# Three stages on one core: every step's place, engine and buffer given by a list instead of by ranks and a planner

## The chip, the core and the metric

The kernel runs on one core of a Trainium2 chip. A core has TensorE (PE in the profile; its weight loads are PEld), VectorE (DVE), ScalarE (ACT), GpSimd (POOL) and SyncE (SP, which only issues transfers). The engines run their own instruction lists in order and wait for each other by semaphores. The metric is the device time of one execution in microseconds (us).

## The reference

Attention whose scores count only where query and key fall into the same bucket (the signs of six projections), and behind it a feed-forward block with an exact GELU:

```python
batch, n_heads, seq, head_dim = (4, 8, 768, 64)
q_bits = (np.einsum('bhsd,dk->bhsk', q, proj) > 0).astype(np.int64)
k_bits = (np.einsum('bhsd,dk->bhsk', k, proj) > 0).astype(np.int64)
mask = q_bucket[:, :, :, None] == k_bucket[:, :, None, :]
scores = scale * np.matmul(q, k.transpose(0, 1, 3, 2))
scores = np.where(mask, scores, -1000000000.0)
scores = scores - np.max(scores, axis=-1, keepdims=True)
attn = np.exp(scores)
attn = attn / (np.sum(attn, axis=-1, keepdims=True) + 1e-09)
attn_out = np.matmul(attn, v)
# x: (B * S, H * D) = (3072, 512); w_in 512 x 2048, w_out 2048 x 512, arriving as 64-bit floats
h = x @ w_in
g = 0.5 * h * (1.0 + erf(h * inv_sqrt2))
out = g @ w_out
```

## The kernel before, in words

The work is cut into 3604 steps. A step is a few instructions of one engine (`emit`), with the steps it needs, the ring of buffers it takes a place from, and the engines on which it may run with a cost for each (`ways`). Some steps, such as a copy or a scaling, may run on VectorE, ScalarE or GpSimd, and a few moves inside SBUF may also be a transfer of SyncE.

Per batch there are 8 heads, two to a pair; per head 6 units of 128 queries. A head's steps load `raw`, round it to `Aq` (L418 or ScalarE's L415, out of `rawe` or `raw`, with the scale `fold`), take what is left over (`Bq`, `Bk`), move halves into `Bk`, `Ak` and `Bq`, project them (L765 to L767 for batch 0, L841 and L842 later), and write the signs as mask rows into `Aq` and `Ak`. A unit is a score product on TensorE (four matmuls, L889, into one of two buffers `s`), a minimum on VectorE (L892), the exponential on ScalarE (L897, into `p`), and then for batch 0 transposes on TensorE with copies into `pt` (L947, L418 or L415), for the other batches the row sum's scaling (`rows<-rows`) and reciprocal (L906), the weights' high half (`hl` or `wbits` from `p`) and low half (L912), and a transposing transfer. The third buffers of `p` and of `hl` are cut out of `wbits`, so their writes carry that name as well. A pair ends with the values' product (L1027 or L1036) and the two halves of `x`.

The weights arrive in pieces, are decoded on VectorE (L527, L532, L537) and scaled. The feed-forward runs in groups of 8 blocks of hidden features for 256 rows: the hidden product (L1239, into one of four buffers `hp`), its evacuation (L1249), GELU (L1274), the high half `g` (L418 or L415) and low half (L1296), and the output product (L1318), then a drain (L1345, L415 or L418) and the store.

The order comes from `Plan.order`, a list planner inside the program: it goes through modelled time with its own costs, hands each free engine the ready step with the lowest rank, and gives a buffer out as it comes free. Ranks are the step's key, a place in the sequence of units shifted by a number of the table `PAR` by the step's kind, class of head and engine. The steps are then emitted in the order of their modelled starts; that order is each engine's instruction list. `flips` and `hashes` are small constants that the heads of batches 1 to 3 use for their masks.

Of the kernel before, what the change touches and what calls it, by code (L numbers as in the profile page):

```python
# [19 lines left out]
P = 128  # L20
TC = 256
# [5 lines left out]
TABLE = 1.39  # L27
CLASSES = ((3, 3, 4, 4, 0, 0, 0, 0), (5, 5, 1, 1, 1, 1, 1, 1), (2, 2, 2, 2, 2, 2, 2, 2))
TURN = 0.11
# [4 lines left out]
PAR = dict(DR_ACT=576.84, DR_DVE=-551.41, SI0=-589.8, SI1=230.04, SI2=-34.64, SI_ACT=-397.26, SI_DVE=-373.75, SI_Pool=-360.2, Z=-61.67, VS0=-433.73, H0=378.62, HL=565.17, VS=-224.84, G2=593.89, HQ=458.56, VQ=-575.62, in0=-255.08, out0=-600, in1=-380.24, out1=295.33, in2=-124.92, out2=-97.71, in3=235.25, out3=-400.5, H1=176.86, H2=542.46, H3=-37.15, H4=458.07, H5=179.41, H6=-511.06, H7=-405.9, MEV=57.33, MGE=-266.31, MSP=582.63, V0=403.75, QK0=240.49, QK1=-248.37, QK2=252.72, MX0=-152.71, MX1=62.08, MX2=-495.94, EX0=75.03, EX1=-181.85, EX2=-102.35, NR0=-144.91, NR1=-247.83, NR2=-577.15, HI0=-417.18, HI1=25.44, HI2=-381.41, LO0=-449.91, LO1=202.06, LO2=376.24, PV0=514.02, PV1=-31.15, PV2=-408.84, TR0=172.3, TR1=-600, TR2=-12.3, V1=-391.11, V2=-325.43, Sin0=526.4, Sin1=-364.12, Sin2=-600, Sin3=277.83, Sout0=-418.02, Sout1=289.1, Sout2=0.64, Sout3=401.64, Lin=-412.45, Pin=231.92, Qin=421.02, Cin=-141.85, Min=-383.86, Lout=-95.97, Pout=107.03, Qout=-175.48, Cout=-318.56, Mout=-147.01, G0=145.57, G1=316.52, G3=502.99, G4=274.38, G5=-52.33, G6=280.57, G7=-451.2, DUP0=-368.48, DUP1=309.05, DUP2=-147.15, LOW0=-74.43, LOW1=400.08, LOW2=-437.3, PRJ0=505.26, PRJ1=-443.97, PRJ2=-573.45, MSK0=-333.44, MSK1=-332.99, MSK2=574.02, DI_ACT=484.2, DI_DVE=198.9, DI_Pool=586.97, WS_ACT=-377.49, WS_DVE=-492.68, WS_Pool=75.03, WH_ACT=-183.8, WH_DVE=254.94, WH_Pool=-132.94, WL_ACT=564.2, WL_DVE=-390.67, WL_Pool=47.05, VH_ACT=332.87, VH_DVE=273.75, VH_Pool=272.39, MV_SP=462.36, MV_ACT=561.02, MV_DVE=187.65, MV_Pool=8.43, LO_ACT=144.07, LO_DVE=-389.23, LO_Pool=-404.23, RND_ACT=-149.62, RND_DVE=-392.64, RND_Pool=-598.96, MSK_ACT=-95.97, MSK_DVE=256.26, MSK_Pool=357.17, HI_ACT=-170.11, HI_DVE=575.2, HI_Pool=368.91, EV_ACT=-392.64, EV_DVE=600, EV_Pool=-334.15, GH_ACT=-383.86, GH_DVE=-207.4, GH_Pool=11.14, RB=-383.49, RS_ACT=406.61, RS_DVE=127.79, RS_Pool=-283.07, XH_ACT=257.16, XH_DVE=206.23, XH_Pool=441.23, XL_DVE=471.07, XL_Pool=-504.86, DUP3=-510.21, DUP4=61.31, DUP5=122.24, EX3=518.86, EX4=293.1, EX5=-530.77, HI3=130.65, HI4=104.05, HI5=600, LO3=-280.76, LO4=-212.73, LO5=56.13, LOW3=-499.53, LOW4=-471.64, LOW5=90.57, MSK3=445.61, MSK4=-85.72, MSK5=-557.26, MX3=-600, MX4=-401.44, MX5=-600, NR3=-216.85, NR4=-574.93, NR5=-600, PRJ3=-473.92, PRJ4=-5.94, PRJ5=1.03, PV3=-599.87, PV4=288.41, PV5=-253.14, QK3=341.47, QK4=536.61, QK5=517.19, SI3=266.44, SI4=573, SI5=-495, TR3=-44.12, TR4=170.66, TR5=-130.38, V3=-546.29, V4=-68.24, V5=-362.38, Linb=-179.56, Loutb=-390.67, Pinb=-106.09, Poutb=-600, Qinb=395.7, Qoutb=248.99, Cinb=-157.9, Coutb=-372.14, Minb=-262.42, Moutb=-159.34, MVf_SP=192.7, MVf_ACT=537.16, MVf_DVE=-141.85, MVf_Pool=6.51, LOf_ACT=319.76, LOf_DVE=-589.84, LOf_Pool=-50.91, RNDf_ACT=600, RNDf_DVE=91.75, RNDf_Pool=-552.12, MSKf_ACT=-231.23, MSKf_DVE=461.34, MSKf_Pool=200.2)  # L34
HOPX = {"PE": -0.04, "DVE": -0.09, "ACT": 0.12, "Pool": 0.03, "SP": 0.88}
# [19 lines left out]
class Plan:  # L55

    HOP = {"PE": 0.2, "DVE": 0.2, "ACT": 0.14, "Pool": 0.07, "SP": 0.03, "none": 0.0}
    ANY = ("hp", "sign")
    SAME = {"PE": 0.0, "DVE": 0.14, "ACT": 0.14}
    START = {"DVE": 4.2, "Pool": 3.3, "SP": 1.2, "ACT": 4.3}
    QUEUE = 2.0  # L70
    PORT = 0.1
    SWITCH = ((0, -0.08, 0.1), (0, 0, 0.1), (0.13, 0.07, 0))
    WINDOW = 3.413
    YIELD = 160.0
    SLACK = {"PE": 0.6, "SP": 1.0}

# [20 lines left out]
    def slack(self, now, of, to_pe):  # L97
        late = now >= self.YIELD and of != "none"
        return late * max(self.SLACK["PE"] * to_pe, self.SLACK["SP"] * (of == "SP"))

    def order(self):
        users, left, ready = {}, {}, {}
        queues = {}
        for s in self.steps:
            left[s] = len(s.needs)
            for n in s.needs:
                users.setdefault(n, []).append(s)
            for e in s.ways:
                ready.setdefault(e, [])
            if s.takes:  # L110
                queues.setdefault(s.takes, []).append(s)
        at = {}
        head = {name: 0 for name in queues}
        waiting = set()
        events = []

        def enlist(s):
            if s.takes in queues and s.takes not in self.ANY and queues[s.takes][head[s.takes]] is not s:
                waiting.add(s)
                return  # L120
            for e in s.ways:
                ready[e].append(s)

        for s in self.steps:
            if not left[s]:
                enlist(s)
        free_at = {e: 0.0 for e in ready}
        free_at.update(self.START)
        dma_at, table = 0.0, "exp"
        port_at, port_of = 0.0, None  # L130
        warm, window, busy = False, 0, {}
        mode = 0
# [1277 lines left out]
```

## Time and profile before

| | us |
|---|---|
| median of 3 runs (lowest, highest) | 868.42 (868.17, 868.68) |
| the profiled execution | 868.76 |
| its span, first to last instruction | 866.8 |
| TensorE busy | 836.1 (96%) |
| VectorE busy | 669.8 (77%) |
| ScalarE busy | 589.2 (68%) |
| GpSimd busy | 214.4 (25%) |

Busy time is that in which at least one instruction of the engine ran; matmuls overlap each other, so a mean duration times a count is more than the busy time. The shares are means over stages with different work, and the section on rows below therefore shows them by stretch.

### The profile page before, as it was taken

The numbers are of one execution on the slowest core, as the hardware profiler recorded it, in microseconds if no ns is written. First come the engines' busy times: TensorE is split into PE (matmuls) and PEld (weight loads), VectorE is DVE, ScalarE is ACT, GpSimd is POOL, SyncE is SP. The second block draws the span as 40 slices with busy tenths as digits, with TensorE's granted clock in tenths as the row PEclk, the third lists the DMA queues.
The fourth block names the chain that finished last, engine by engine and source line by source line (L and its number), as shares of the span: only waits on it lengthen the run. The fifth ranks groups of instructions, "written<-read, shape, count | busy, mean of one in ns | idle before, by whom it ended". The sixth has DMA issues, their size and how long they took to land.

```text
span 866.8 us, 16831 instructions
## 1 busy us (share of the span) xinstructions
PE 836.1 (96%) x6428; PEld 608.4 (70%) x6428; DVE 669.8 (77%) x1285; ACT 589.2 (68%) x1012; POOL 214.4 (25%) x232
## 2 busy tenths in 40 slices
PE   4898998999999999999999999999999999999998
PEld 2675766776777686887777677777767877676663
DVE  6999989999999999978998998798978752212122
ACT  5888887777788878787877868667868642223321
POOL 4543231313431315222212214214225300000000
PEclk9999999999999999999999999999999999999999
DMA  7755453564597999788988798788877970000000
GB/s 253 218 194 162 126 152 98 152 149 107 119 198 153 195 177 206 162 149 151 198 173 159 173 177 172 148 170 169 172 167 128 152 152 2 25 1 25 2 25 24
DMA packets 271439, 119.91 MB, mean 138 GB/s; under 512 B 228928, under 2 KB 253504, under 8 KB 271360
## 3 DMA queue, kind: packets, MB, share of 16 engines
q1 hardware_dynamic: 271104, 118.85, 62.7%
q8 instruction: 50, 0.82, 0.4%
q14 instruction: 29, 0.24, 0.1%
q10 hardware_dynamic: 256, 0.00, 0.0%
HBM read 41.95 MB, written 6.29 MB: 56 GB/s over the span
## 4 chain that ended last, share of the span: by engine, by line
PE 64%; DVE 2%; DMA 0%; ACT 0%; issue 0%; DVEq 0%; ACTq 0%
PE hp L1318 24%; PE hp L1239 23%; PE s L889 9%; PE hp L1036 7%; PE hp L842 1%; PE hp L841 1%; DVE s L892 1%; DMA pt<-wbits 0%; DVE wbits L912 0%; DVE hl L912 0%; DVE Bq L819 0%; DVE g L418 0%; DVE vhl L689 0%; ACT L897 0%; ACT p L897 0%
## 5 line engine op out<-in xcount | busy, mean ns | idle before, releaser
L1239 PE MATMUL hp<-x,Win 128*128 128x256 f16 x2304 | 268.2, 273 | 0.5 <-DVE o L1345 0.3
L1318 PE MATMUL hp<-Wout,g 128*128 128x512 f16 x1152 | 266.8, 380 | 0.2 <-DVE g L1296 0.2
L1239 PEld LDWEIGHTS <-Win 128*128 128x128 f16 x2304 | 219.5, 98 | 41.9 <-issue 13.2
L892 DVE TENSOR_SCALAR_CACHE_REDUCE s<-s 128x768 f32<-128x768 f32 x192 | 182.1, 963 | 17.9 <-PE s L889 17.5
L1318 PEld LDWEIGHTS <-g 128*128 128x128 f16 x1152 | 106.2, 98 | 125.3 <-issue 13.4
L897 ACT ACTIVATE p<-s,rows 128x768 f32<-128x768 f32 x147 | 132.3, 901 | 48.4 <-DVE s L892 25.0
L889 PE MATMUL s<-Ak,Aq 128*128 128x384 f32 x360 | 138.2, 384 | 6.6 <-ACT p L897 6.1
L1249 ACT ACTIVATE h<-hp,ffs 128x512 f32<-128x512 f32 x96 | 65.6, 684 | 102.6 <-PE hp L1239 102.0
L889 PE MATMUL s<-Bk,Bq 128*128 128x384 f32 x360 | 121.4, 337 | 0.0
L418 DVE TENSOR_SCALAR g<-h,ffs 128x512 f16<-128x512 f32 x36 | 19.3, 537 | 96.0 <-PE hp L1318 78.1
L1296 DVE SCALAR_TENSOR_TENSOR g<-h,ffs,g 128x512 f16<-128x512 f32 x96 | 72.5, 771 | 25.9 <-ACT g L415 23.8
L889 PEld LDWEIGHTS s<-Ak,Aq 128*128 128x128 f32 x360 | 68.0, 189 | 22.1 <-ACT p L897 14.0
L1036 PE MATMUL hp<-pt,vhl 128*64 128x256 f16 x1296 | 76.1, 274 | 0.0
L1036 PEld LDWEIGHTS <-vhl 128*64 128x64 f16 x1296 | 68.6, 110 | 8.7 <-issue 8.0
L889 PEld LDWEIGHTS s<-Bk,Bq 128*128 128x128 f32 x360 | 68.3, 190 | 1.1
L912 DVE SCALAR_TENSOR_TENSOR wbits<-p,rows,wbits 128x768 f16<-128x768 f32 x60 | 62.5, 1046 | 3.8 <-POOL wbits L418 2.9
L897 ACT ACTIVATE wbits<-s,rows 128x768 f32<-128x768 f32 x45 | 40.4, 898 | 11.2 <-DVE s L892 5.6
L1274 ACT ACTIVATE h<-h 128x2048 f32<-128x2048 f32 (+1 forms) x25 | 46.1, 1843 | 0.4
L947 PE MATMUL hp<-ident,p 128*128 128x128 f32 x288 | 40.8, 275 | 2.6 <-DVE pt L418 1.9
L912 DVE SCALAR_TENSOR_TENSOR hl<-p,rows,hl 128x768 f16<-128x768 f32 x39 | 39.3, 1012 | 1.5 <-POOL hl L418 1.2
L947 PEld LDWEIGHTS hp<-ident,p 128*128 128x128 f32 x288 | 32.9, 141 | 8.1 <-DVE pt L418 2.5
L415 ACT ACTIVATE pt<-hp 128x384 f32<-128x384 f32 x75 | 33.8, 490 | 6.5 <-PE hp L947 6.2
(194 smaller groups left out, 1099.0 us busy)
## 6 DMA issues: line engine op xcount, KB each, us to landing
raw<-qk SPq DMA_DIRECT2D x28, 384.0 KB, 4.0
vraw<-v SPq DMA_DIRECT2D x28, 384.0 KB, 4.1
wbits<-w_in SPq DMA_DIRECT2D x16, 512.0 KB, 4.7
wbits<-w_out SPq DMA_DIRECT2D x16, 512.0 KB, 4.5
out<-o SPq DMA_DIRECT2D x11, 512.0 KB, 3.0
Bq<-Aq SPq DMA_DIRECT2D x22, 192.0 KB, 2.9
Bk<-Bq SPq DMA_DIRECT2D x18, 192.0 KB, 3.1
Bk<-Aq SPq DMA_DIRECT2D x17, 192.0 KB, 2.9
```

The costliest lines, as they stand in the source:

```text
L415: nc.scalar.activation(out=out, in_=in_, func=func, scale=scale, bias=bias)
L889: nc.tensor.matmul(to, x, y, start=k == 0, stop=k == 1)
L892: nc.vector.tensor_scalar(out=both(sp), in0=both(sp), scalar1=BIG / 2, scalar2=None, op0=ALU.min, op1=ALU.min, accum_out=nb,)
L897: nc.scalar.activation(out=buf(ex).rearrange("p (b k) -> p b k", b=2), in_=both(sp), func=AF.Exp, scale=-1.0, bias=nb, accum_out=sums[:, t ...
L912: nc.vector.scalar_tensor_tensor(out=buf(hi)[:, 1], in0=buf(ex), scalar=r, in1=buf(hi)[:, 0], op0=ALU.mult, op1=ALU.subtract,)
L947: nc.tensor.transpose(buf(step[0])[:, (k - k0) * P : (k - k0 + 1) * P], buf(ex)[:, words(k)], ident32,)
L1036: nc.tensor.matmul(pv[j * D : (j + 1) * D], buf(vh)[:, tv, kt, j * D : (j + 1) * D], buf(holds[j][0])[:, tp * KT + kt, :nt], start=kt == 0 ...
L1239: nc.tensor.matmul(buf(pair[0])[:, j * ch[1] : (j + 1) * ch[1]], win_hl[:, f0 // WB1, tw, pr, f0 % WB1 : f0 % WB1 + P], x[:, tx, pr, : ch[1]],
L1249: nc.scalar.activation(out=bufs["h"][0][:, 2 * fp : 2 * fp + 2, :nt], in_=buf(pair[0])[:, : 2 * nt].rearrange("p (j k) -> p j k", j=2), fu ...
L1274: nc.scalar.activation(out=h, in_=h, func=AF.Gelu)
L1296: nc.vector.scalar_tensor_tensor(out=gt[:, 1, s2, :nt], in0=h[:, s2, :nt], scalar=sg, in1=gt[:, 0, s2, :nt], op0=ALU.mult, op1=ALU.subtract,)
L1318: nc.tensor.matmul(buf(banks[u]), gt[:, tg, f, u * P : (u + 1) * P], wout_hl[:, ft // UT, tw, ft % UT], start=fresh and f == ti == 0, stop ...
```

## The change

`PAR`, its shifts and the whole of the planner's simulation go. In their place stands `ORDER`, a text of three characters for each of the 3604 steps: two give the step's place, one its engine and the number of its buffer. `Plan.order` reads it, sorts the steps by place and checks that each comes behind what it needs and that its buffer is free. The steps, their instructions and what they need are the same; where each stands, and on which of its engines, is another.

```diff
-PAR = dict(DR_ACT=576.84, DR_DVE=-551.41, SI0=-589.8, ...)
+ENGINES = ("PE", "DVE", "ACT", "Pool", "SP", "none")
+CODE = "ABCDEFGHIJKLMNOPQRSTUVWXYZabcdefghijklmnopqrstuvwxyz0123456789+-"
+ORDER = (
+    "CKYASIAEgAXCAagAyAA1gBMABPgBpABwIB4ICCACJICZICmICtIBigADgAIIALQAJQANQAKIAMIAOoAVBAZQAPAAWQAbQAcIAgAAlIApQAuoA2AA8QA0DA4Q"
...
     def order(self):
-        users, left, ready = {}, {}, {}
-        queues = {}
+        assert len(ORDER) == 3 * len(self.steps)
         for s in self.steps:
...
+            high, low, way = (CODE.index(c) for c in ORDER[3 * s.seq : 3 * s.seq + 3])
+            s.start = 64 * high + low
+            s.engine = ENGINES[way // 8]
+            s.cost = s.ways[s.engine][0]
+            s.slot = way % 8 if s.takes else None
+        steps = sorted(self.steps, key=lambda s: s.start)
...
-        sp = add("PE", 0.785, scores, t - PAR[f"QK{cl}"], made, takes="s")
-        mx = add("DVE", 0.876, least, t - PAR[f"MX{cl}"], [sp])
+        sp = add("PE", 0.785, scores, t, made, takes="s")
+        mx = add("DVE", 0.876, least, t, [sp])
```

The lines of the changed kernel have lower numbers; by the kernel before, its L375 is L418 (a scaling or copy of `affine`), L396 is L439, L441 is L484, L484 is L527, L685 is L728, L776 is L819, L849 is L892, L863 is L906, L869 is L912 and L1017 is L1060.

VectorE at the start of the program, before. `Aq_89` is the first head's rounded operand, `rawe` its data, `flips` the constants out of the transfer `off`, `Bq` and `Bk` what is left over, and `Win` the first weights:

```order
L370 TENSOR_SCALAR praw<-praw 128x6
L373 CAST first_hi<-praw 128x12
L375 TENSOR_TENSOR first_lo<-praw,first_hi 64x12 x2
L484 TENSOR_SCALAR flips<-off 64x1
L484 TENSOR_SCALAR flips<-flips 32x1 x3
L418 TENSOR_SCALAR Aq_89<-rawe_121,fold 128x768
L439 TENSOR_TENSOR Bk_92<-rawe_121,Aq_89 64x768
L728 SCALAR_TENSOR_TENSOR Bq_91<-rawe_121,Aq_89 64x768
L439 TENSOR_TENSOR Bk_96<-raw_80,Aq_93 64x768
L728 SCALAR_TENSOR_TENSOR Bq_95<-raw_80,Aq_93 64x768
L527 TENSOR_SCALAR Win<-wbits 128x1024
```

The same place of VectorE's list now:

```order
L327 TENSOR_SCALAR praw<-praw 128x6
L330 CAST first_hi<-praw 128x12
L375 TENSOR_SCALAR Aq_89<-rawe_121,fold 128x768
L332 TENSOR_TENSOR first_lo<-praw,first_hi 64x12 x2
L685 SCALAR_TENSOR_TENSOR Bq_91<-rawe_121,Aq_89 64x768
L396 TENSOR_TENSOR Bk_92<-rawe_121,Aq_89 64x768
L375 TENSOR_SCALAR Aq_93<-raw_80,fold 128x768
L441 TENSOR_SCALAR flips<-off 64x1
L441 TENSOR_SCALAR flips<-flips 32x1 x3
L396 TENSOR_TENSOR Bk_96<-raw_80,Aq_93 64x768
L685 SCALAR_TENSOR_TENSOR Bq_95<-raw_80,Aq_93 64x768
L375 TENSOR_SCALAR Ak_90<-sign_72 12x768
```

The rounding of the first head moved ahead of `first_lo` and `flips`, the second head's came over from ScalarE, and the mask row `Ak_90` from GpSimd stands ahead of the decoding.

VectorE in the middle of the program, before, in the stretch that leads to the left-over part `Bq0` of one head. `wbits` and `hl` are halves of the attention weights, `rows` the row sums, `s0` and `s1` the score buffers:

```order
L892 TENSOR_SCALAR s1_63,rows_99<-s1_63 128x2x384
L892 TENSOR_SCALAR s0_62,rows_99<-s0_62 128x2x384
L912 SCALAR_TENSOR_TENSOR wbits_61<-p0_68,rows_99,wbits_61 128x768
L906 RECIPROCAL rows_99<-rows_99 128x1 x2
L418 TENSOR_SCALAR hl0_70<-wbits_61,rows_99 128x768
L418 TENSOR_SCALAR Aq0_89<-raw0_80,fold_130 128x768
L912 SCALAR_TENSOR_TENSOR hl0_70<-wbits_61,rows_99,hl0_70 128x768
L819 SCALAR_TENSOR_TENSOR Bq0_91<-raw0_80,fold_130,Aq0_89 128x768
```

The same place now:

```order
L375 TENSOR_SCALAR wbits_61<-wbits_61,rows_99 128x768
L375 TENSOR_SCALAR rows_99<-rows_99 128x1
L863 RECIPROCAL rows_99<-rows_99 128x1
L375 TENSOR_SCALAR hl0_70<-p1_69,rows_99 128x768
L869 SCALAR_TENSOR_TENSOR wbits_61<-wbits_61,rows_99 128x768
L869 SCALAR_TENSOR_TENSOR hl0_70<-p1_69,rows_99,hl0_70 128x768
L863 RECIPROCAL rows_99<-rows_99 128x1
L849 TENSOR_SCALAR s1_63,rows_99<-s1_63 128x2x384
L869 SCALAR_TENSOR_TENSOR wbits_61<-p0_68,rows_99,wbits_61 128x768
L776 SCALAR_TENSOR_TENSOR Bq0_91<-raw0_80,fold_130,Aq0_89 128x768
```

High halves (`TENSOR_SCALAR` into `wbits` and `hl`) and a scaling of `rows` stand among VectorE's own work. They came from GpSimd, whose list has 84 rows instead of 224; its last rows before the final branch were these:

```order
L418 TENSOR_SCALAR Aq1_93<-sign0_72,flips_157 12x768
L418 TENSOR_SCALAR Ak1_94<-sign0_72,flips_157 12x768
L418 TENSOR_SCALAR wbits_61<-p1_69,rows_99 128x768
L418 TENSOR_SCALAR wbits_61<-wbits_61,rows_99 128x768
L418 TENSOR_SCALAR hl1_71<-p1_69,rows_99 128x768
```

and are now these, which stand much earlier in the program:

```order
L375 TENSOR_SCALAR Ak1_94<-sign0_72,flips_157 12x768
L375 TENSOR_SCALAR rows_99<-rows_99 128x1
L375 TENSOR_SCALAR g_1656<-h_1655,ffs_108 128x512
L375 TENSOR_SCALAR hl1_71<-wbits_61,rows_99 128x768
L375 TENSOR_SCALAR Bq0_91<-Aq0_89 64x768
```

Of GpSimd's work behind the attention of batch 0 little is left; its work up to there is nearly what it was.

## Rows read from the trace of the kernel before

**Rows 1.** Busy time by stretch: start:end length, busy us (instructions) by engine, clock, DMA.

```profile
6.00:164.00 158.00, 138.62 (x996) 102.34 (x997) 147.92 (x285) 129.14 (x264) 54.65 (x53) 1.00 0.53 166
164.00:700.00 536.00, 534.28 (x4268) 397.08 (x4268) 481.34 (x933) 412.04 (x689) 156.64 (x164) 1.00 0.83 165
700.00:868.00 168.00, 163.18 (x1167) 109.01 (x1165) 38.54 (x63) 46.51 (x58) 0.01 (x1) 1.00 0.10 26
```

**Rows 2.** Chain that ended last, one piece: start us, us, what.

```profile
401.84 1.41 PE s L889 x8
```

**Rows 3.** Busy time of four pieces of 50 us.

```profile
200.00:250.00 50.00, 49.41 (x394) 35.99 (x393) 46.84 (x99) 37.69 (x65) 20.11 (x20) 1.00 0.61 123
250.00:300.00 50.00, 49.37 (x386) 35.97 (x384) 48.26 (x92) 41.20 (x67) 12.99 (x14) 1.00 0.90 180
300.00:350.00 50.00, 49.85 (x394) 35.72 (x393) 47.44 (x92) 39.01 (x73) 18.11 (x16) 1.00 0.91 190
...
400.00:450.00 50.00, 49.96 (x398) 37.77 (x395) 47.91 (x94) 37.82 (x69) 10.13 (x12) 1.00 0.88 174
```

**Rows 4.** Start, in order of time: start us, us, engine line op, tiles.

```profile
0.74 0.40 SPq L707 DMA_DIRECT2D rawe<-qk  x1
...
5.67 0.17 DVE L373 CAST first_hi<-praw 128x12 fp32r<-128x12 f32 x1
...
7.88 0.15 DVE L484 TENSOR_SCALAR flips<-off 64x1 f32<-64x1 f32 x1 [1.60 <-DMA off<-offset]
...
8.57 0.62 DVE L418 TENSOR_SCALAR Aq<-rawe,fold 128x768 fp32r<-128x768 f32 x1
...
16.22 0.52 PE L889 MATMUL s<-Ak,Aq 128*128 128x384 f32 x1
```

**Rows 5.** Instructions on tile rawe until 8 us: landing of its transfer.

```profile
DMA to landing us min/median/max: 3.5/3.5/3.5
```

**Rows 6.** VectorE's groups until 164 us: shapes xcount, busy us, mean ns, idle before.

```profile
L418 DVE TENSOR_SCALAR pt<-hp 128x384 f32<-128x384 f32 x21 | 11.2, 548 | 0.7 <-PE hp L548 0.5 <-PE hp L947 0.2
```

**Rows 7.** VectorE's groups of the whole span.

```profile
L1296 DVE SCALAR_TENSOR_TENSOR g<-h,ffs,g 128x512 f16<-128x512 f32 x96 | 72.5, 771 | 25.9 <-ACT g L415 23.8
...
L912 DVE SCALAR_TENSOR_TENSOR wbits<-p,rows,wbits 128x768 f16<-128x768 f32 x60 | 62.5, 1046 | 3.8 <-POOL wbits L418 2.9 <-ACT wbits L415 0.6
...
L418 DVE TENSOR_SCALAR g<-h,ffs 128x512 f16<-128x512 f32 x36 | 19.3, 537 | 96.0 <-PE hp L1318 78.1 <-ACT h L1274 17.8
...
L418 DVE TENSOR_SCALAR wbits<-p,rows 128x768 f16<-128x768 f32 x17 | 10.4, 614 | 0.5 <-DMA pt<-wbits 0.4
...
L418 DVE TENSOR_SCALAR Ak<-sign,flips 12x768 fp32r<-12x768 f32 x6 | 5.2, 868 | 0.2
...
L418 DVE TENSOR_SCALAR rows<-rows 128x1 f32<-128x1 f32 x34 | 5.0, 148 | 8.3 <-ACT p L897 6.0 <-ACT wbits L897 1.8
...
L418 DVE TENSOR_SCALAR Bk<-Bq 64x768 fp32r<-64x768 f32 x1 | 0.6, 557 | 0.0
```

**Rows 8.** Lines L912 and L1296 behind 30 us: ns min/median/max, first and last start.

```profile
L912 DVE SCALAR_TENSOR_TENSOR wbits<-p,rows,wbits x60: 991/1014/1633, 222.7 to 704.6; 128x768 f16<-128x768 f32 x60
...
L1296 DVE SCALAR_TENSOR_TENSOR g<-h,ffs,g x96: 730/746/1396, 176.3 to 853.2; 128x512 f16<-128x512 f32 x96
```

**Rows 9.** End, in order of time.

```profile
847.54 0.49 DVE L418 TENSOR_SCALAR g<-h,ffs 128x512 f16<-128x512 f32 x1 [14.39 <-PE hp L1318]
847.94 1.41 DVE L1296 SCALAR_TENSOR_TENSOR g<-h,ffs,g 128x512 f16<-128x512 f32 x2
...
863.22 0.69 ACT L415 ACTIVATE o<-hp,ffs 128x512 f32<-128x512 f32 x1 [15.40 <-PE hp L1318]
```

**Rows 10.** TensorE from 330 to 347 us, in order of time.

```profile
334.40 1.47 PE L1318 MATMUL hp<-Wout,g 128*128 128x512 f16 x6
...
336.40 2.76 PE L1318 MATMUL hp<-Wout,g 128*128 128x512 f16 x12
...
339.70 2.12 PE L1318 MATMUL hp<-Wout,g 128*128 128x512 f16 x9
```

More of the change, by code (lines that the diff above doesn't have):

```diff
@@ new lines, in order @@
+            high, low, way = (CODE.index(c) for c in ORDER[3 * s.seq : 3 * s.seq + 3])
[4 more added lines that the diff above has]
+        steps = sorted(self.steps, key=lambda s: s.start)
+        free = {(name, k) for name, slots in self.rings.items() for k, _ in slots}
+        for s in steps:
+            assert all(n.start < s.start for n in s.needs), (s.seq, "comes before what it needs")
+            if s.takes:
+                free.remove((s.takes, s.slot))
+            for hold in s.frees:
+                hold["left"] -= 1
+                if not hold["left"]:
+                    free.add((hold["holder"].takes, hold["holder"].slot))
@@ L233, in tile_bucket_attention_moe @@
+        return steps
 @with_exitstack
@@ L430, in affine_on @@
         return {
-            e: (affine_cost(e, n, pointer) + more - less * (e == "Pool"), PAR[f"{name}_{e}"]) for e in ("ACT", "DVE", "Pool")
+            e: (affine_cost(e, n, pointer) + more - less * (e == "Pool"), 0.0) for e in ("ACT", "DVE", "Pool")
         }
     def subtract_on(name, n):
-        return {e: (subtract_cost(e, n), PAR[f"{name}_{e}"]) for e in ("DVE", "Pool")}
+        return {e: (subtract_cost(e, n), 0.0) for e in ("DVE", "Pool")}
     def subtract(engine, out, in0, in1):
@@ L515, in load @@
                     )
-                loads.append(add("SP", 1.93, load, key + d * step - PAR["L" + name], takes="wraw"))
+                loads.append(add("SP", 1.93, load, key + d * step, takes="wraw"))
             def decode(n_op, f=f, loads=loads):
@@ L692, in low @@
             )
-        raw = add("SP", 1.43, load, key - PAR["VQ"], takes="vraw")
+        raw = add("SP", 1.43, load, key, takes="vraw")
         hi = add(affine_on("VH", S, True), 0, high, key, [raw, scaled], takes="vhl", port=True)
@@ L733, in add_low @@
             if scale:
[L734 removed]
+                return add("DVE", subtract_cost("DVE", S), scaled, key, [hi], port=True)
             box = []
@@ L745, in head_early @@
         top, end = slice(0, D), slice(D, P)
-        raw = add("SP", 1.43, load, key - PAR["HQ"], takes="rawe" if b == 0 and h % 2 == 0 else "raw")
+        raw = add("SP", 1.43, load, key, takes="rawe" if b == 0 and h % 2 == 0 else "raw")
         hi = add(affine_on(f"RND{first}", S, True), 0, high, key, [raw, *clear], port=True)
@@ L821, in low @@
             )
-        raw = add("SP", 1.43, load, key - PAR["HQ"], takes="rawe" if b == 0 and h % 2 == 0 else "raw")
+        raw = add("SP", 1.43, load, key, takes="rawe" if b == 0 and h % 2 == 0 else "raw")
         hi = add(affine_on(f"RND{first}", S, True), 0, high, key, [raw, *clear], port=True)
-        lo = add("DVE", subtract_cost("DVE", S), low, key + PAR[f"LOW{cl}"], [hi], port=True)
+        lo = add("DVE", subtract_cost("DVE", S), low, key, [hi], port=True)
         free(raw, [lo])
@@ L851, in sign @@
                 )
-            box.append(add("PE", 0.08 + 0.92e-3 * (c1 - c0), project, key + PAR[f"PRJ{cl}"], [space, hashed], takes="hp"))
+            box.append(add("PE", 0.08 + 0.92e-3 * (c1 - c0), project, key, [space, hashed], takes="hp"))
             products += box
-            below = add("ACT", affine_cost("ACT", c1 - c0), lower, key + PAR[f"PRJ{cl}"], box[:1])
-            signs.append(add("DVE", subtract_cost("DVE", c1 - c0) - 0.07, sign, key + PAR[f"PRJ{cl}"], [below], port=True))
+            below = add("ACT", affine_cost("ACT", c1 - c0), lower, key, box[:1])
+            signs.append(add("DVE", subtract_cost("DVE", c1 - c0) - 0.07, sign, key, [below], port=True))
             free(box[0], signs[-1:])
```

322 lines of the change are left out of this document (136 added, 186 removed).

## The prediction

> **What bounds the kernel now.** I read the stretches first, then the start instruction by instruction, then the groups by line. The stretches [rows 1] show three stages. From 6 to 164 us (the attention of batch 0, ahead of the first hidden product) VectorE is busy 147.92 of 158 us and TensorE only 138.62: VectorE carries this stage, and 19.4 of TensorE's idle microseconds lie here. From 164 to 700 us TensorE is busy 534.28 of 536 us: it idles 1.7 us, at the full granted clock, so there is nothing to win in it by order alone. VectorE is busy 481.34 us (90%) there, ScalarE 412.04, GpSimd 156.64. After 700 us only the feed-forward products are left, TensorE has no gap before its last matmul, and behind that stand a drain of 0.69 us at 863.22 [rows 9] and its store, and both orders end with such a pair. So a new order can win in the first stage alone, and it can lose in the second, where a late VectorE, ScalarE or transfer becomes a gap on TensorE that nothing covers.
>
> **What the change does.** TensorE has the same 10,998 rows, in another order. 140 instructions leave GpSimd (rows of the order: 224 to 84), 121 rows more stand on VectorE, 50 on ScalarE; 19 transfers inside SBUF leave SyncE's queue for an engine. Counted up to the first hidden product on TensorE, VectorE has 230 instructions instead of 240 there; what GpSimd gives up it gives up almost wholly behind that point.
>
> **First stage, the start.** VectorE finishes its cast at 5.84 us, then makes two small corrections and waits for a tiny transfer before `flips`, which starts at 7.88; the first rounding of a head, `Aq`, starts at 8.57 [rows 4]. The head's data were issued at 0.74 [rows 4] and took 3.5 us to land [rows 5], so at 4.2 us they were there. In the new order `Aq` stands right behind the cast, and `flips`, whose first reader is a head of batch 1, comes after the second head's `Aq`. `Aq` can start at about 5.85: 2.7 us earlier. Behind it hang the moves, the projection, the signs and the first score matmul, at 16.22 us [rows 4]; in the new order only one head is projected ahead of it, so it should come at least as much earlier. I take 2.7 us.
>
> **First stage, VectorE's load.** Eight copies of transposed weights (`pt`, 548 ns each [rows 6]) go from VectorE to ScalarE: 8 x 0.548 = 4.4 us. ScalarE idles 158 - 129.14 = 28.9 us in the stage [rows 1] and takes them. The other edits are a few short forms each way, which I cost at nothing and leave 1.5 us of either sign for. Together 7.1 us, if VectorE bound the stage at every moment. It idles 10.1 us in it, so I take 6. Bounds: 12 us won, if half of that idle time goes too; 2 us lost, if the copies on ScalarE hold up exponentials that the next scores wait for.
>
> **Second stage, VectorE's load.** Moved onto VectorE, at the durations of [rows 7]: 43 scalings of a row sum at 148 ns, 6.4 us; 17 weights' high halves (`wbits<-p`) at 614, 10.4 us; 18 more of the same form from or into other buffers, 11.1 us; 31 operand moves, masks and roundings of 768 elements, between 557 and 868 ns, taken at 650, 20.2 us; five `g` at 537, 2.7 us; against it two output drains that leave, at 0.69 us [rows 9] 1.4 us. Sum 49 us. Two things come off. Neighbouring instructions overlap: three whose single durations are 0.49, 0.75 and 0.75 us stand from 847.54 to 849.35, 1.81 us instead of 1.99 [rows 9], some 0.09 us a joint. At 0.08 us for 119 instructions more this is 9 us. And VectorE's instructions are stretched where GpSimd works beside them: L912's commonest form has a median of 1014 and a mean of 1046 ns, with a longest of 1633; L1296 has 746, 771 and 1396 [rows 7, 8]. Mean less median, times the counts, is 60 x 0.032 + 96 x 0.025 = 4.3 us for these two; with the three other forms of L912 and `g` I take 8 us, most of which goes with GpSimd's work. So VectorE's need in the stage is about 481 + 49 - 9 - 8 = 513 us of 536, 96%; 530 at the most, 500 at the least.
>
> The Trainium skill ("SBUF — State Buffer", Who interferes with whom) says that a VectorE instruction in a two-port mode, or with two SBUF inputs, and a GpSimd instruction shut each other out for a whole instruction. The trace agrees in direction: 1.63 us against a median of 1.01 [rows 8]. By that rule some of VectorE's idle time before instructions would go as well, and its need would be nearer 500 than 513 us; by the rows it is 513. The forecast is the same by both, since TensorE sets the stage's end; only the chance of the slower rival would halve.
>
> **What 96% costs TensorE.** The kernel before has stretches like that. In the four 50 us pieces where VectorE is busiest (46.84, 48.26, 47.44 and 47.91 us) TensorE idles 0.59, 0.63, 0.15 and 0.04 us [rows 3]: 1.41 of 200 us. Over 536 us this makes 3.8 us; 1.7 are there already, so the stage becomes 2 us longer. Bounds: at the worst piece's rate 6.8, which is 5 longer; at the best's 0.4, which is 1 shorter.
>
> **Changes of kind on TensorE.** Counted in its two orders, TensorE goes 386 instead of 319 times from one kind of product to another, since scores come singly between shorter runs of feed-forward products. From 334.40 to 336.40 stand six output products and four score matmuls, from 336.40 to 339.70 twelve and four [rows 10]: six products are 1.30 us, so four score matmuls with the way there and back are 0.70. Eight in one piece take 1.41 [rows 2]. A change costs nothing that shows; I take 0, at most 0.02 us each, 1.3 us.
>
> **Transfers.** Nineteen fewer moves lie in SyncE's queue, ahead of transposes that TensorE reaches many microseconds later; VectorE and ScalarE pay for them above. At the start the third piece of weights is now issued behind loads that wait for their buffers; its reader, the second decoding, stands behind five minimum searches on VectorE in both orders. I cost both at nothing; if that cover failed, the second decoding would wait, and with it a sum of squares that no score waits for.
>
> **Sum.** Against the profiled execution, 868.76 us (span 866.8 and 1.96 around it): -6 in the first stage, +2 in the second, 0 elsewhere: 864.8. That execution stands 0.34 above the median, 868.42; so 864.4 against the median.
>
> **Rivals.**
> - *The load takes the place of the order (slower).* VectorE becomes the bound between 164 and 700 us. The busiest piece of the trace shows what it reaches, 48.26 of 50 us, 96.5% [rows 3]; 536 us at that rate hold 517 us of work. Above 517 the stage grows: at 530 (no relief from GpSimd, little overlap) to 549, 13 us, and with the 6 us of the first stage the kernel ends at +7; at 525 to 544, +2. In its middle about 872. For it: every piece of the stage, not one in three, would be this dense, and the score chain (matmul, VectorE's minimum, exponential, buffer free) has two score buffers only. Against it: 513 lies below 517, and GpSimd's stretching goes. The Trainium skill ("Perfetto Trace Analysis", Optimizing Scalar/DVE Operations) advises to take work off a saturated VectorE, to ScalarE or even GpSimd; the change goes the other way. By that advice the result is this rival's; in the trace VectorE at 96% cost TensorE 0.63 of 50 us at the most. Chance 0.25.
> - *No difference.* The first stage gains 3 and the second loses 3: within 0.2% of 868.4. For it: both terms are a few microseconds and of opposite sign. Chance 0.17.
> - *The first stage gains all it can.* 7.1 us and half of VectorE's 10.1 us of idle time there, and the second stage loses nothing: 856.5. For it: scores come singly and are spread, so that VectorE finds the next one ready; against it: something of the idle time is the chain's own. Chance 0.13.
> - That the list doesn't do what it says I give no chance: the instructions' order shows it.
>
> **How the numbers follow.** The forecast, 864.4, has 0.45 and its own range 860.5 to 866.5 (gain of 4 to 9, loss of 1 to 5, not both ends at once). A change below 0.2%, 1.7 us, can hardly be told from none here. Faster: 0.45 + 0.13 = 0.58; same 0.17; slower 0.25. The range that leaves 2 in 10 out goes down to the fullest gain's edge, 857, and up to the slower rival a little beyond its middle, 873.
>
> **What would show it.** In the changed kernel's profile: `Aq` on VectorE before 6.5 us and the first score matmul by 13.5; the first hidden product at 156 to 160 us instead of 164; after it VectorE busy 500 to 520 us in as long a stretch, GpSimd under 30, L1296's mean near 750 ns; TensorE's gaps there 2 to 6 us together, ended mostly by VectorE's or ScalarE's score steps. I would be wrong in the first stage if the first hidden product doesn't come earlier, in the second if TensorE's gaps behind it sum to over 7 us, or to under 1.

## The result and the profile after

The changed kernel takes 874.24 us (median; 873.06 to 874.81) against 868.29 (867.66 to 868.68) for the kernel before: ratio 1.0067, 95% interval 1.0050 to 1.0085, so 5.8 us slower where 4 us faster was forecast. Its profiled execution took 874.51 us, its span 872.7.

The stretches of the changed kernel (length; busy us and instructions of PE, PEld, DVE, ACT and POOL; granted clock; DMA share; GB/s), which answer to [rows 1]:

```profile
6.00:164.00 158.00, 139.52 (x986) 104.50 (x987) 140.73 (x274) 128.38 (x267) 47.79 (x49) 0.96 0.58 166
164.00:700.00 536.00, 531.87 (x4250) 393.63 (x4250) 495.10 (x1031) 451.86 (x735) 17.78 (x18) 1.00 0.76 155
700.00:868.00 168.00, 168.00 (x1192) 111.98 (x1191) 48.20 (x84) 54.14 (x71) 0.00 (x0) 1.00 0.14 34
```

TensorE's gaps in the second stretch are as forecast: 536 - 531.87 = 4.1 us. The first stretch is not as forecast. VectorE, which carried it, is busy 7 us less than before, yet TensorE is only 0.9 us further, at a clock of 0.96. The start went as forecast (VectorE and TensorE in order of time; start, length), as against 8.57 and 16.22 in [rows 4]:

```profile
5.88 0.62 DVE L375 TENSOR_SCALAR Aq<-rawe,fold 128x768 fp32r<-128x768 f32 x1
...
12.82 0.66 PE L846 MATMUL s<-Ak,Aq 128*128 128x384 f32 x1 [2.08 <-DVE Ak L375]
```

So what was won by then is lost between 13 and 164 us. The waits from 30 to 170 us (what waited, for what; us in total, times, longest) name it:

```profile
ACT sign L727 <- PE hp L724: 8.9, 3, 8.4
...
DVE Wout L484 <- DMA wbits<-w_out: 7.5, 1, 7.5
...
PE hp L722 <- DVE rb L1023: 7.1, 1, 7.1
```

The longest wait of each line belongs to one event. VectorE in order of time, and below it TensorE:

```profile
46.18 0.95 DVE L685 SCALAR_TENSOR_TENSOR Bq<-raw,Aq 64x768 fp32r<-64x768 f32 x1
54.60 0.69 DVE L484 TENSOR_SCALAR Wout<-wbits 128x1024 int32<-128x1024 int32 x1 [7.47 <-DMA wbits<-w_out]
55.21 0.16 DVE L375 TENSOR_SCALAR sums<-sums 128x4 f32<-128x4 f32 x1
55.28 0.48 DVE L1023 SCALAR_TENSOR_TENSOR rb<-hp,s_v,rb 128x256 f32<-128x256 f32 x1
```

```profile
48.27 0.49 PE L904 MATMUL hp<-ident,p 128*128 128x128 f32 x3
55.82 0.65 PE L722 MATMUL hp<-Aq,first_lo 128*44 128x512 f32 x1 [7.06 <-DVE rb L1023]
```

A decoding of weights (L484) stands on VectorE ahead of `rb`, which empties a buffer `hp` that TensorE wants next. Nobody needs the decoded weights soon; all that stands behind the decoding is late. And the clock falls (stretches of 4 us, columns as above):

```profile
48.00:52.00 4.00, 0.76 (x6) 0.49 (x4) 0.00 (x0) 0.87 (x2) 1.55 (x1) 0.89 1.07 254
52.00:56.00 4.00, 0.18 (x1) 0.18 (x2) 1.40 (x5) 0.00 (x0) 0.00 (x0) 0.50 0.14 53
56.00:60.00 4.00, 4.00 (x16) 2.04 (x17) 4.00 (x7) 1.94 (x4) 0.00 (x0) 0.50 0.14 43
60.00:64.00 4.00, 4.00 (x32) 2.77 (x29) 1.91 (x4) 2.11 (x5) 0.00 (x0) 0.83 0.89 249
```

After TensorE has stood idle, 4 us and more of its work run at 0.50, the lower of its two levels (1.2 of 2.4 GHz). A smaller stop of the same sort follows at 102.7 us (clock 0.72 from 104 to 108), behind another decoding's second part (VectorE in order of time):

```profile
100.28 1.23 DVE L489 SCALAR_TENSOR_TENSOR Win<-wbits,Win 128x1024 int32<-128x1024 int32 x1 [1.69 <-DMA wbits<-w_out]
```

This one decodes `w_in` and waits for a piece of `w_out`, which it doesn't read.

**Which transfer did the decoding wait for?** It reads two pieces of `wbits`. SyncE's queue issued them and others so (start, length):

```profile
42.33 0.37 SPq L470 DMA_DIRECT2D wbits<-w_in  x1
42.74 0.47 SPq L671 DMA_DIRECT2D Bq<-Aq  x1
43.32 0.53 SPq L578 DMA_DIRECT2D vraw<-v  x1
43.94 0.76 SPq L664 DMA_DIRECT2D rawe<-qk  x1
44.75 0.48 SPq L671 DMA_DIRECT2D Ak<-Aq  x1
45.29 0.58 SPq L470 DMA_DIRECT2D wbits<-w_out  x1
```

The landings of the first and the last (KB, us from issue to landing):

```profile
wbits<-w_in SPq DMA_DIRECT2D x1, 512.0 KB, 4.9
...
wbits<-w_out SPq DMA_DIRECT2D x1, 512.0 KB, 9.3
```

The decoding's own last piece is the one issued at 42.33, landed at 42.33 + 4.9 = 47.2. The one it waited for, landed at 54.6, is a piece of the next decoding. `wbits` has three places. By ORDER this decoding's pieces lie in places 0 and 2, the next one's in place 1, between them, and the decoding reads them through one strided view:

```
halves = wbits.rearrange("p (s f t) -> p s f t", f=512, t=2)[:, at : a + b - at + 1 : abs(a - b)]
```

With a step of 2 the view's range takes in place 1, and the instruction list has three transfers to wait for, where the decoding before it has two:

```
L484 TENSOR_SCALAR Wout<-wbits 128x1024 [waits DMAHW6_49,DMAHW4_49]
L484 TENSOR_SCALAR Wout<-wbits 128x1024 [waits DMAHW7_49,DMAHW4_49,DMAHW1_49]
```

(the third decoding, and the fourth, which is the one at 54.60). Both kernels have five decodings with places 0 and 2. In the kernel before, all five have three transfers in their lists too, but the piece between had always landed in time: this is the longest wait of a decoding for a transfer (VectorE's waits; us in total, times, longest):

```profile
DVE Wout L527 <- DMA wbits<-w_in: 0.2, 1, 0.2
```

In the changed kernel three of the five have a transfer into place 1 issued shortly before or among their parts.

### The profile page after: what moved, and what is told of

Read it like the earlier page. It is cut to its first block, busy times and chain, and to the rows that moved or that the text cites. A ratio compares the mean times of both kernels' runs of the same rounds, so it can differ in the third digit from the quotient of the medians.

```text
span 872.7 us, 16560 instructions
## 1 busy us (share of the span) xinstructions
PE 840.2 (96%) x6428; PEld 610.3 (70%) x6428; DVE 686.7 (79%) x1394; ACT 635.9 (73%) x1073; POOL 68.5 (8%) x81
## 4 chain that ended last, share of the span: by engine, by line
PE 78%; DVE 10%; ACT 5%; DMA 3%; issue 2%; POOL 0%; SPq 0%; ACTq 0%; DVEq 0%; POOLq 0%
PE hp L1196 26%; PE hp L1275 24%; PE s L846 12%; PE hp L993 7%; PE hp L984 3%; DVE s L849 3%; PE hp L904 2%; ACT p L854 2%; DMA pt<-wbits 1%; DMA wbits<-w_out 1%; DVE wbits L869 1%; DVE hl L869 1%; PE hp L798 1%; PE hp L799 1%; ACT pt L372 1%
## 5 line engine op out<-in xcount | busy, mean ns | idle before, releaser
L1275 PE MATMUL hp<-Wout,g 128*128 128x512 f16 x1152 | 276.3, 380 | 0.0
L1196 PE MATMUL hp<-x,Win 128*128 128x256 f16 x2304 | 272.7, 273 | 0.0
L849 DVE TENSOR_SCALAR_CACHE_REDUCE s<-s 128x768 f32<-128x768 f32 x192 | 183.1, 958 | 16.1 <-PE s L846 14.7
L1275 PEld LDWEIGHTS <-g 128*128 128x128 f16 x1152 | 104.3, 98 | 116.2 <-issue 17.6
L846 PE MATMUL s<-Ak,Aq 128*128 128x384 f32 x360 | 143.9, 400 | 8.6 <-ACT p L854 5.2
L1253 DVE SCALAR_TENSOR_TENSOR g<-h,ffs,g 128x512 f16<-128x512 f32 x96 | 70.2, 744 | 38.3 <-ACT g L372 37.2
L375 DVE TENSOR_SCALAR g<-h,ffs 128x512 f16<-128x512 f32 x41 | 19.4, 478 | 74.4 <-ACT h L1231 56.4
L869 DVE SCALAR_TENSOR_TENSOR wbits<-p,rows,wbits 128x768 f16<-128x768 f32 x57 | 57.6, 1012 | 1.3 <-ACT wbits L372 0.6
L904 PE MATMUL hp<-ident,p 128*128 128x128 f32 x288 | 43.6, 280 | 3.1 <-ACT pt L372 1.8
L869 DVE SCALAR_TENSOR_TENSOR hl<-p,rows,hl 128x768 f16<-128x768 f32 x41 | 41.5, 1015 | 2.2 <-ACT hl L372 1.8
L372 ACT ACTIVATE g<-h,ffs 128x512 f16<-128x512 f32 x50 | 35.3, 715 | 10.2 <-PE hp L1275 10.0
L372 ACT ACTIVATE pt<-hp 128x384 f32<-128x384 f32 x83 | 37.7, 491 | 4.9 <-PE hp L904 4.3
```

The costliest lines, as they stand in the source:

```text
L372: nc.scalar.activation(out=out, in_=in_, func=func, scale=scale, bias=bias)
L846: nc.tensor.matmul(to, x, y, start=k == 0, stop=k == 1)
L849: nc.vector.tensor_scalar(out=both(sp), in0=both(sp), scalar1=BIG / 2, scalar2=None, op0=ALU.min, op1=ALU.min, accum_out=nb,)
L869: nc.vector.scalar_tensor_tensor(out=buf(hi)[:, 1], in0=buf(ex), scalar=r, in1=buf(hi)[:, 0], op0=ALU.mult, op1=ALU.subtract,)
L904: nc.tensor.transpose(buf(step[0])[:, (k - k0) * P : (k - k0 + 1) * P], buf(ex)[:, words(k)], ident32,)
L1196: nc.tensor.matmul(buf(pair[0])[:, j * ch[1] : (j + 1) * ch[1]], win_hl[:, f0 // WB1, tw, pr, f0 % WB1 : f0 % WB1 + P], x[:, tx, pr, : ch[1]],
```

## Experiments

Theory A: a wait for a piece that isn't read, with the clock's fall behind it, takes what the first stage had won. Rivals: B, VectorE's load (the wait only shows where a full engine runs late); C, the burst of transfers; D, for the second stage, TensorE's own order. Differences between runs below are differences of their ratios to the kernel before, times 868.3 us. The interval of one ratio is 0.8 to 1.6 us to either side, so such a difference is good to some 2 us.

**1. Other buffer numbers.**

```diff
 # places of the two pieces that each decoding reads, in the order of the decodings
-(0,1) (1,2) (0,1) (0,2) (2,1) (2,0) (0,2) (2,1) (0,1) (2,1) (1,0) (2,1) (0,1) (2,0) (2,0) (0,1)
+(0,1) (1,2) (0,1) (1,2) (1,0) (1,2) (0,1) (1,2) (0,1) (2,1) (1,0) (2,1) (0,1) (2,1) (1,0) (1,2)
```

> The changed kernel with other buffer numbers for the raw weight pieces and nothing else: same order, same engines. Each decoding then reads two neighbouring pieces of wbits (0 and 1, or 1 and 2), never 0 and 2. Theory A, a wait for a piece that isn't read: in the changed kernel the decoding at 54.60 us waits for three transfers, the third of them into the piece that lies between its own two; its own last piece had landed 4.9 us after its issue at 42.33, at 47.2. Without that wait VectorE goes on at about 47.3, TensorE doesn't stop for 7.06 us, its clock stays at 1.00, and the smaller stop at 102.7 to 105.4 shrinks: 874.2 - 7.1 - 4.1 (the busy time that the lower clock added) - 1 to 2, and 0 to 3 given back, so 861 to 865. Theory B, VectorE's load: the wait only shows where a full engine runs late, and another wait takes its place: 870 to 875. Theory C, the burst of six transfers at 42 to 46 us is too much at once, whoever waits: 868 to 873, with a wait of 3 us or more for raw, vraw or a weight piece before 60 us.

Measured: 864.8 us, ratio 0.9958 (0.9945 to 0.9970), 9.5 under the changed kernel. The fourth decoding now has two transfers in its list of waits, and starts at once, with the same six transfers issued 0.5 us later than before (VectorE; TensorE's next wait; the first stretch):

```profile
47.69 1.05 DVE L484 TENSOR_SCALAR Wout<-wbits 128x1024 int32<-128x1024 int32 x1
```

```profile
50.87 0.43 PE L722 MATMUL hp<-Aq,first_lo 128*44 128x512 f32 x1 [1.58 <-DVE rb L1023]
```

```profile
6.00:164.00 158.00, 146.54 (x1075) 111.00 (x1076) 152.95 (x293) 137.03 (x283) 47.90 (x50) 1.00 0.62 176
164.00:700.00 536.00, 531.44 (x4215) 390.03 (x4213) 493.70 (x1029) 451.62 (x731) 16.20 (x17) 1.00 0.76 154
```

VectorE is 12 us busier in the first stretch than in the changed kernel and TensorE 7.0, at full clock. For the first stage A holds; B and C, which left the wait or moved it, fall.

**2. The wait filled.** Everything waits as in the changed kernel, but TensorE has something to do.

```diff
         for s in steps:
+            if s.seq == 335:
+                for _ in range(9):
+                    plan.steps[187].emit()
             s.emit()
```

> The changed kernel with 36 more TensorE matmuls (the scores of one tile, nine times again, into a bank that nobody reads any more) put where TensorE stands still at 48.8 to 55.8 us: about 36 x 0.18 = 6.4 us of a wait of 7.06. Every wait stays as it was. It prices the clock alone. If TensorE's clock falls because it stood still, the clock stays at 1.00 there and the time falls by what half speed cost after 55.8 us: some 2.5 to 3.5 us, to 870.5 to 872. If the clock costs nothing that ends up in the time, or falls for another reason: 873.5 to 875.

Measured: 869.26, ratio 1.0012 (1.0003 to 1.0021): 36 matmuls that nobody reads make the kernel 4.8 us faster, more than expected. VectorE still waits, and TensorE's clock stays up:

```profile
53.37 0.69 DVE L484 TENSOR_SCALAR Wout<-wbits 128x1024 int32<-128x1024 int32 x1 [6.23 <-DMA wbits<-w_out]
```

```profile
52.00:56.00 4.00, 4.00 (x24) 3.41 (x22) 2.63 (x6) 0.00 (x0) 0.00 (x0) 1.00 0.04 15
56.00:60.00 4.00, 4.00 (x38) 2.88 (x38) 4.00 (x7) 3.54 (x7) 0.00 (x0) 1.00 0.48 107
```

So a TensorE that stands still is what lowered the clock, and not the wait as such. Two things swell the 4.8: the decoding's wait ended 1.2 us earlier in this profile, and the second stop, at 104 to 108 us, is nearly gone too (3.79 of 4 us busy, clock 1.00). From the busy time of the changed kernel and run 1, which have the same matmuls in the same order (840.2 and 837.1), half speed cost 3.1 us in all.

**3. The first wait alone.** Run 1, with the changed kernel's places for the first five decodings, so that of all the decodings only the fourth has places 0 and 2.

```diff
-(0,1) (1,2) (0,1) (1,2) (1,0) (1,2) (0,1) ...
+(0,1) (1,2) (0,1) (0,2) (2,1) (1,0) (0,1) ...
```

> The run with other buffer numbers (864.8 us) with the changed kernel's own numbers put back for five pairs of pieces up to the one that waited, so that only the decoding at 54.60 us has pieces 0 and 2 and waits for the transfer into piece 1; all later decodings keep neighbouring pieces. It prices that one wait, and what stays for the other two such decodings. If nearly all of the 9.4 us between the changed kernel (874.2) and that run hang on the one wait (7.06 us of TensorE and half speed after it, by the matmuls that filled it about 5): 870 to 874. If the second stop, at 102.7 to 105.4 us, had a large part of its own: 868 to 870. If the wait is harmless alone: 864 to 866.

Measured: 870.99, ratio 1.0026 (1.0016 to 1.0036): 5.9 us over run 1, 3.6 under the changed kernel. So put back alone the one wait costs 5.9, and 3.6 are left for the others; "nearly all" it is not.

```profile
54.70 0.69 DVE L484 TENSOR_SCALAR Wout<-wbits 128x1024 int32<-128x1024 int32 x1 [7.14 <-DMA wbits<-w_out]
```

**4. The transfer moved behind.** The changed kernel's own places; SyncE's list:

```diff
 L671 DMA Ak_90<-Aq_89 64x768
-L470 DMA wbits<-w_out 128x1024
 L578 DMA vraw_81<-v 128x6x128
+L470 DMA wbits<-w_out 128x1024 [waits DVE]
 L470 DMA wbits<-w_out 128x1024
```

> The changed kernel with its own buffer numbers and one step moved: the transfer into piece 1 (w_out, issued at 45.29 us) stands behind the third part of the decoding that waited for it, so that this decoding waits for its own two pieces only and the transfer is issued when it has ended. Theory A: another cure of the same wait, 863.5 to 867.5, though the next decoding's piece comes some 5 us later. If the wait for w_out was one for a busy queue or a late piece and not for the place of the buffer: 870 and more, since the transfer is now later still. If the next decoding (at 68.19 us) then waits for it: 867.5 to 870.

Measured: 866.68, ratio 0.9979 (0.9962 to 0.9996). A later transfer, and 7.6 us less: the wait was one for a place, not for a busy queue. The decoding starts at 47.70 as in run 1. Taken away alone, the one wait is thus worth 7.6 us, where put back alone it cost 5.9 (run 3); the others make 1.9 to 3.6.

**5. The first stage of before, the second of after,** and **6. the first stage of after (with the places of run 1), the second of before.** Both are lists put together at the first hidden product.

> The kernel before in the whole first stage (order, engines and buffers up to the first hidden product), the changed kernel's order and engines from there on. It prices the second stage alone. Theory A puts the loss in the first stage: the second stage costs the 2 to 2.5 us that TensorE's gaps grow by (from 1.7 to 4.1 us after 160 us), so 869.5 to 871.5 beside 868.3 for the kernel before. Theory B (VectorE 92 to 96 per cent busy in the second stage is the loss): 872.5 to 875. If the second stage costs nothing: 868 to 868.8.

> The changed kernel's first stage with the buffer numbers of the first of these runs (no decoding that waits for a piece it doesn't read), and the kernel before's order and engines from the first hidden product on. Theory A: the time of that first run less the 2 to 2.5 us of the second stage: 858.5 to 863, under both kernels. Theory B: the second stage was the loss, so about 868, and 4 or more below the first run. Theory C: 866 to 871.

Measured: 874.91, ratio 1.0076 (1.0063 to 1.0088), and 860.3, ratio 0.9912 (0.9898 to 0.9927), the fastest of all, 7.6 us under the kernel before. The second stage of after costs 4.0 us behind its own first stage (runs 1 and 6) and 6.6 behind that of before, where 2 to 2.5 was expected; run 5 falls into the range that was given for B. But 2.0 of the 6.6 lie ahead of its first hidden product, which starts at 165.96 us instead of 163.95, half of it in a stop at the seam of the two lists (run 5):

```profile
165.96 2.23 PE L1196 MATMUL hp<-x,Win 128*128 128x256 f16 x19 [0.98 <-DVE rb L1023]
```

The stretches from 164 to 700 us of runs 5 and 6:

```profile
164.00:700.00 536.00, 530.54 (x4243) 392.58 (x4241) 494.37 (x1023) 449.00 (x731) 17.29 (x18) 1.00 0.77 155
```

```profile
164.00:700.00 536.00, 534.39 (x4274) 396.04 (x4273) 480.00 (x930) 410.44 (x689) 155.87 (x160) 1.00 0.82 163
```

Gaps of 5.5 us against 1.6 in this stretch. The rest is busy time: TensorE is busy 838.1 us in all in run 5 and 836.1 before, 837.1 in run 1 and 835.2 in run 6, 2.0 more each time for the same matmuls. Counted in the traces of runs 1 and 6 behind 164 us, TensorE goes 498 and 386 times from one kind of product (hidden, output, score, value, projection and a few small ones) to another. If all of the 2.0 us were the price of these 112 changes, a change would cost 18 ns. The traces show otherwise. TensorE in run 5, in order of time:

```profile
267.24 1.46 PE L1275 MATMUL hp<-Wout,g 128*128 128x512 f16 x6
...
268.35 0.52 PE L846 MATMUL s<-Ak,Aq 128*128 128x384 f32 x1
...
269.24 0.82 PE L1275 MATMUL hp<-Wout,g 128*128 128x512 f16 x3
269.99 0.19 PEld L846 LDWEIGHTS s<-Ak,Aq 128*128 128x128 f32 x1 [0.43 <-ACT wbits L854]
269.99 0.44 PE L846 MATMUL s<-Ak,Aq 128*128 128x384 f32 x1
...
270.80 0.82 PE L1275 MATMUL hp<-Wout,g 128*128 128x512 f16 x3
```

Six output products and four score matmuls take 2.00 us, as in [rows 10]. The next three and four take 1.56, where by the prediction's figures (1.30 us for six, 0.70 for four) they would take 1.35. The score product's weight load waits for ScalarE's exponential until 269.99, and since the output products end at 270.06 no gap shows: the wait counts as busy time. Such waits have grown (weight loads of score products, 164 to 700 us; of run 6, then of run 1):

```profile
PEld s L846 <- ACT p L854: 1.7, 4, 0.7
PEld s L846 <- ACT wbits L854: 1.4, 3, 0.7
```

```profile
PEld s L846 <- ACT p L854: 6.4, 9, 1.7
PEld s L846 <- ACT wbits L854: 4.7, 11, 1.0
```

An estimate, from the kernel before and run 5, which from the first hidden product on have the same 5,433 matmul records with 389 and 500 changes, each distance between two starts held against the median of its kind: 2.8 us more of gaps, 0.8 of covered waits, and 0.7 for the changes, 6 ns each. The other 0.5 us of busy time lie ahead of the first hidden product.

**7. and 8. Order and engines of the second stage parted.** Run 1 with the engines of before behind the first hidden product; run 6 with those of after.

> The run of the changed kernel with other buffer numbers (864.8 us), its order kept everywhere, but from the first hidden product on every step on the engine that it has in the kernel before (GpSimd back, some 170 pieces of work off VectorE and ScalarE). Of the 4.5 us by which that run is over the one with the second stage of before (860.3), 2.3 are TensorE's gaps and 2.0 are busy time of the same matmuls. Theory B, engines: VectorE's load makes the gaps, so they shrink by about 2: 862 to 863.5. Theory D, order: gaps and busy time both come from the order of TensorE's own work: 864 to 865.5. If an order made for one set of engines doesn't fit the other: over 866.

> The other half: the run with the second stage of before (860.3 us), its order kept everywhere, but from the first hidden product on every step on the engine that it has in the changed kernel (GpSimd nearly idle). Theory B, engines: the gaps come with the engines: 862 to 863.5. Theory D, order: 860 to 861. If order and engines don't fit each other: over 864, with gaps of 4 us and more after 160 us.

Measured: 888.69, ratio 1.0246 (1.0232 to 1.0260), and 915.97, ratio 1.0559 (1.0545 to 1.0574). Both went the third way, far beyond what I had thought of: TensorE idles 20.7 and 36.9 of the 536 us.

```profile
164.00:700.00 536.00, 515.27 (x4047) 374.96 (x4047) 452.50 (x883) 389.40 (x659) 150.06 (x153) 1.00 0.77 156
```

```profile
164.00:700.00 536.00, 499.07 (x3855) 356.51 (x3854) 465.39 (x953) 415.58 (x678) 23.04 (x16) 1.00 0.71 143
```

No engine is full: VectorE is busy less than in either whole kernel. Presumably what a step waits for now stands behind other work on its new engine; no run shows that by itself. So these runs don't tell engines from order as the source of the second stage's gaps; that stays open.

**9. The start undone.** Run 6 with the four writes of `flips` ahead of the first `Aq`.

```diff
+L441 TENSOR_SCALAR flips<-off 64x1
+L441 TENSOR_SCALAR flips<-flips 32x1 x3
 L375 TENSOR_SCALAR Aq_89<-rawe_121,fold 128x768
```

> The run with the second stage of before (860.3 us) with one step moved back: VectorE's four writes of flips stand ahead of the first Aq again, as in the kernel before, and wait there for the transfer of off until about 7.9 us. If the 2.7 us of the start go through to the end: 862.5 to 863.3. If the first stage has slack that takes them up: 860 to 861, with TensorE's gaps to 160 us no larger than the 11.1 us of that run.

Measured: 862.55, ratio 0.9939 (0.9927 to 0.9952), 2.3 us over run 6. `Aq` starts at 8.78, the first score matmul at 15.24 instead of 12.87: the 2.4 us of the start go through to the end, within the noise of such a difference.

**10. The copies undone.** Run 6 with `pt<-hp` of the first stage on its engines of before (16 from ScalarE to VectorE, 8 the other way).

> The run with the second stage of before (860.3 us) with the copies out of TensorE's transposes (pt<-hp) in the first stage on the engines that they have in the kernel before: 16 go back to VectorE and 8 to ScalarE, 8 net, 4.4 us more on VectorE. If VectorE's load sets the first stage (the second term of the sum): 3 to 4.4 us more, 863.3 to 864.7. If the gain came from the order alone: 860 to 861.

Measured: 864.62, ratio 0.9966 (0.9952 to 0.9979), 4.7 us over run 6: the time lies in the range that was given for VectorE's load, the difference a little above it (VectorE's groups until 164 us; of run 10, then of run 6):

```profile
L375 DVE TENSOR_SCALAR pt<-hp 128x384 f32<-128x384 f32 x21 | 11.4, 549 | 0.1
```

```profile
L375 DVE TENSOR_SCALAR pt<-hp 128x384 f32<-128x384 f32 x13 | 7.0, 547 | 0.1
```

Some of the 4.7 is the clock. In the profiled execution (865.96 us) TensorE stands still for 2.05 us before 51.91 us, where run 6 shows 1.58, and its next work runs at 0.57:

```profile
52.00:56.00 4.00, 4.00 (x19) 2.13 (x21) 4.00 (x6) 2.07 (x4) 0.00 (x0) 0.57 0.48 136
```

Two of the five executions have a mean clock of 0.998; the three at 1.000 took 863.65 to 864.62 us, some 4 us over run 6. And since other engines in a fixed order can cost by themselves (runs 7 and 8), VectorE's load is the likely cause and not the only possible one.

## Why the prediction was wrong

By the runs the change is a sum of three: the first stage without the false waits, -7.6 us (run 6 against before); the second stage, +4.0 (run 1 against run 6); the false waits, +9.5 (the changed kernel against run 1). Together +5.9, and the comparison gave 5.8; they must agree, since each step starts where another ends, so this doesn't confirm the parts. Taken the other way round, with the second stage of after (runs 1 and 5), the first stage gives -10.2 and the second +6.6: the parts are not independent of each other. The prediction had -6, +2 and nothing.

- **The step that failed** is the one on transfers, "I cost both at nothing; if that cover failed, the second decoding would wait, and with it a sum of squares that no score waits for". It was the fourth decoding, and the error has two parts. I looked at the order of the transfers and not at the numbers of their buffers, which the list also gives. And I priced a wait by who reads its result, where on an engine that runs its list in order the price is what stands behind it: `rb`, then a buffer of TensorE's. One such wait cost 5.9 us by itself (run 3) and 7.6 in the changed kernel (run 4), all of them 9.5 (run 1).
- **The clock** had no term. [Rows 1] show it at 1.00 throughout, so a stop that changes it has no row there. Half speed makes 3.1 of the 9.5 us. The Trainium skill ("TensorE: Matmul & The Clock Gate", HAM oscillation — how this bites in real kernels) names waits for transfers as what throws TensorE back to its lower clock. The trace agrees, 0.50 behind the 7.06 us, and run 2 adds that the wait does it only where TensorE has nothing else to do.
- **The start**: forecast 2.7, measured 2.3 (run 9). **VectorE's load in the first stage**: the eight copies were put at 4.4, and run 10 gives 4.7. Of the whole stage I took 6 and 7.6 came, inside the bounds of 12 and -2: about the 7.1 of the two terms, and the 0.5 above it is less than the noise. My own test of this stage, the first hidden product at 156 to 160 us, failed in the changed kernel (164.6); in run 1 (154.1) it comes earlier still.
- **The second stage**: VectorE's need was put at 513 us, 500 at the least, and is 495. I had counted rows of the lists; by the instructions of the two pages 151 leave GpSimd, and 109 and 61 come to VectorE and ScalarE. Summed by form over the two traces from 164 to 700 us, VectorE gets 98 instructions more, 39 us at their old durations (taken: 119, 49 us), overlap takes off 8 (taken: 9), and 18 go because the instructions are shorter (taken: 8). GpSimd's stretching went altogether: L1253, which is L1296 before, had a mean of 771 and a longest of 1396 ns [rows 7, 8], and has now:

```profile
L1253 DVE SCALAR_TENSOR_TENSOR g<-h,ffs,g x96: 729/745/752, 180.8 to 859.6; 128x512 f16<-128x512 f32 x96
```

By the rule of the Trainium skill that the prediction gave ("SBUF — State Buffer", Who interferes with whom: a VectorE instruction in a two-port mode, or with two SBUF inputs, and a GpSimd instruction shut each other out) the need was nearer 500 than 513, and the 495 lie on that side. TensorE's gaps, 4.1 us, lie in the forecast 2 to 6, and ScalarE's score step ends most of them (from 164 to 700 us):

```profile
PE s L846 <- ACT p L854: 2.6, 4, 1.2
PE s L846 <- ACT wbits L854: 1.0, 2, 0.5
```

The term was +2 and is +4.0. Run 1 has 3.0 us more of gaps than run 6 in this stretch, and busy time makes the rest. **Changes of kind**, taken at 0 with a bound of 1.3, are an estimated 0.7 of it (run 5), inside the bound, though I counted 67 more where the traces show 112. The step that fell short is "What 96% costs TensorE": it read gaps alone from pieces of the old order, and a score product that waits under the end of an output product leaves none. These waits, like the gaps, are for ScalarE's exponential. ScalarE is busy 451.86 us in this stretch instead of 412.04, which had no term; whether its load, VectorE's or the order makes it late stays open.

- **The rivals**: the slower one had the sign and the wrong place. VectorE isn't the bound of the second stage. Without the false waits the forecast's sum holds nearly to the microsecond (864.4; run 1 864.8), but by luck: two errors of 1.6 and 2 us, each no larger than the noise of such a difference, cancel.

The version to keep is that of run 6, with the new first stage, neighbouring places for each decoding, and the old second stage.

## What to carry to other kernels

Where a change hands out buffers anew, read the waits of each instruction and not only the order: a strided view over a shared tile waits for everything that lands inside its range. Price a new wait by what is queued behind it on its engine, and then by the clock of a TensorE that stands still. And a fixed order belongs to its choice of engines: changing one without the other cost up to 56 us here (run 8 against run 6).

## What was not expected of the hardware

36 matmuls without a reader, put into a stop of 7 us, made the whole kernel 4.8 us faster, in good part since the work behind the stop ran at a granted clock of 1.00 instead of 0.50. And a transfer issued last in a burst of six (2,176 KB) took 9.3 us to land where the first took 4.9.
